# State times K and Q of a head in one 128-column block, and rows turned by VectorE from chunk 5 on

## The chip, the core and the metric

The kernel runs on one core of a Trainium2 chip. The core has five engines that follow their own instruction queues in order and wait for each other through semaphores: TensorE (matrix products, PE in the profile; its weight loads, which overlap the products, are PEld), VectorE (DVE), ScalarE (ACT), GpSimd (POOL) and SyncE (SP), which here issues nearly all DMAs. The metric is the device time of one execution in microseconds; a single execution has been profiled, and the times of three others are given as a median.

## What is computed

A delta-rule attention layer in float32 (4 batches, 8 heads, 768 steps, head size 48) feeds a gated feed-forward layer over 3072 tokens (model width 384, inner width 1536):

```python
for t in range(S):
    kt, vt, bt = (k_n[:, :, t], v[:, :, t], beta[:, :, t, None])
    y[:, :, t] = np.einsum('bhd,bhde->bhe', q[:, :, t], state)
    v_old = np.einsum('bhde,bhd->bhe', state, kt)
    state = state + bt[:, :, :, None] * np.einsum('bhd,bhe->bhde', kt, vt - v_old)
...
x = np.ascontiguousarray(attn_out.transpose(0, 2, 1, 3)).reshape(B * S, H * D)
...
rms = np.sqrt(np.mean(x * x, axis=-1, keepdims=True) + 1e-06)
xn = x / rms * rms_g
g = xn @ w_gate
silu = g * (1.0 / (1.0 + np.exp(-g)))
val = xn @ w_val
return (silu * val @ w_out).astype(np.float32)
```

`k_n` is k divided by its norm.

## The kernel before

The 768 steps are cut into 12 chunks (`NCH`) of 64 steps (`C`). The 32 pairs of batch and head lie as 16 columns of pairs, in two halves of the 128 partitions. For each chunk `c` the kernel runs these stages:

- `norms(c)` and `prep(c)`: the norms of K, K scaled (L816), K turned so that the head's dimension lies on the partitions (`kt`; from chunk 5, `KVEC`, by a trip through DRAM and a VectorE transpose of 32x32 blocks, L819 to L828; before that by TensorE transposes, L537), the scores of K with itself (`scores`, L560) and the inverse of a triangular matrix in 32x32 pieces (L865 to L930, with scaling by beta on GpSimd from chunk 4 on). Two merge products (L971, L991) join the pieces in `mt`; between them stands `zz`, which borrows a part of `yn`.
- `qpart(c)`: Q turned into `qt` (L625) and its scores with K (`pt`).
- `recur(c)`: the state times K (`on_state(kt)`, L1029) is taken from V into `r_` (L1058); the state times Q (`on_state(qt)`, the same line) is copied into `yn` (L1066). Then `mt` times `r_` gives `u_` (L1092), and `u_` gives both the second part of the output (`pu`, L1106) and the growth of the state (`ku`, L1163). `yn` is summed (L1194), its mean square taken (L1200), and scaled (L1233). TensorE turns it in three 128x128 transposes for each of two row groups (L1239), and ScalarE copies it with the factor `rms_g` into `xf` (L1248). Seven VectorE sums of `xf`'s parts follow (L1263).
- `ffn(c)`: from chunk 2 on, 30 groups of products (L1406) by a scheme with fewer products, with sums on VectorE and ScalarE (L1416 to L1423), and then `down` with seven products (L1463). Chunks 0 and 1 use plain products (`ffn_plain`, L1311 and `down_mm`, L1293). `xf` can be written for the next chunk once the last L1406 product has read it.

A matmul on a part of the array names its rows by the partitions of its operands and its columns by the partitions of its output. In `on_state` each product has 48 rows (one head's dimension, lower or upper half of the partitions by `d`) and 64 stationary columns (64 steps), with output on the lower or upper half by `bb`: four tiles of 64x64. Two neighbouring half columns of `kt` or `qt` belong to the heads `g` = 0 and 1.

What sets the order is a list. Each operation is added to a `Plan` with its engine, an estimated duration and the keys that it reads and writes. `ORDER` is a string of two digits per operation that names the sequence, and `Plan.run` writes the instructions of all engines out in that sequence; PSUM banks are handed out (`Group`) in the same walk. So each engine's queue is fixed when the program is built; the durations steer the hand-out of banks and the fillers at the start, and nothing at run time.

SyncE issues its DMAs one after the other; one that waits for its data holds up those behind it.

## Time and profile before

| what | value |
|---|---|
| median of three runs | 669.61 us (667.61 to 669.8) |
| the profiled execution, own time | 669.93 us |
| its span, first to last instruction | 668.2 us |
| granted TensorE clock | 0.999 |
| busy in the span: TensorE, its loads, VectorE, ScalarE, GpSimd | 656.6, 606.7, 530.3, 299.3, 147.5 us |
| records of L1029 (matmuls of the state with K or Q) | 704 + 640 |
| records of L1239 (transposes of yn) | 72 |
| instructions in the span | 23232 |

Busy times overlap between engines and do not add up. Each float32 matmul shows up as two records of matmul and two of weight load; a transpose leaves one. A record's duration holds its latency, so that records that follow each other closely overlap, and what a block of them costs is seen from the start of one block to the start of the next.

### The profile page before, as it was taken

The numbers are of one execution on the slowest core, as the hardware profiler recorded it, in microseconds if no ns is written. First come the engines' busy times: TensorE is split into PE (matmuls) and PEld (weight loads), VectorE is DVE, ScalarE is ACT, GpSimd is POOL, SyncE is SP. The second block draws the span as 40 slices with busy tenths as digits, with TensorE's granted clock in tenths as the row PEclk, the third lists the DMA queues.
The fourth block names the chain that finished last, engine by engine and source line by source line (L and its number), as shares of the span: only waits on it lengthen the run. The fifth ranks groups of instructions, "written<-read, shape, count | busy, mean of one in ns | idle before, by whom it ended". The sixth has DMA issues, their size and how long they took to land.

```text
span 668.2 us, 23232 instructions
## 1 busy us (share of the span) xinstructions
PE 656.6 (98%) x9970; PEld 606.7 (91%) x9970; DVE 530.3 (79%) x1139; ACT 299.3 (45%) x729; POOL 147.5 (22%) x204
## 2 busy tenths in 40 slices
PE   8989999999999999999999999999999999999997
PEld 5777787787899999999999999999999999999997
DVE  5888999888789798798898798698789699458263
ACT  4676734235246246346245346345345255245230
POOL 2211332032600600610710510610501401000000
PEclk9999999999999999999999999999999999999999
DMA  8489855766555176265356276174373601200101
GB/s 217 94 312 258 204 143 81 130 128 107 132 81 104 41 120 117 49 105 88 57 94 103 46 126 111 29 129 67 71 116 49 115 15 27 41 18 2 24 2 24
DMA packets 259799, 63.07 MB, mean 94 GB/s; under 512 B 248880, under 2 KB 251952, under 8 KB 259376
## 3 DMA queue, kind: packets, MB, share of 16 engines
q1 hardware_dynamic: 258656, 61.39, 46.7%
q8 instruction: 78, 1.28, 0.8%
q10 hardware_dynamic: 1040, 0.20, 0.2%
q14 instruction: 25, 0.20, 0.1%
HBM read 46.61 MB, written 18.87 MB: 98 GB/s over the span
## 4 chain that ended last, share of the span: by engine, by line
PE 93%; DVE 3%; issue 1%; ACT 1%; DMA 1%; POOL 0%; SPq 0%; POOLq 0%; ACTq 0%; DVEq 0%
PE bank L1406 41%; PE bank L1463 21%; PE bank L1311 9%; PE bank L1293 4%; PE bank L1029 3%; PE bank L560 3%; PE bank L1106 2%; PE bank L1092 2%; PE bank L779 1%; PE bank L1239 1%; PE bank L1163 1%; PE bank L798 1%; PE bank L1574 1%; PE bank L971 1%; PE bank L991 1%
## 5 line engine op out<-in xcount | busy, mean ns | idle before, releaser
L1406 PE MATMUL bank<-xf,w_in 128*128 128x128 f32 x1440 | 178.3, 276 | 0.3 <-ACT tmp L1418 0.3
L1406 PEld LDWEIGHTS bank<-xf,w_in 128*128 128x128 f32 x1440 | 169.4, 192 | 1.6 <-ACT tmp L1418 0.5
L1416 DVE TENSOR_TENSOR tmp<-tmp,bank 128x512 f32<-128x512 f32 x180 | 120.3, 682 | 48.5 <-PE bank L1406 35.8
L1406 PE MATMUL bank<-xf,more 128*128 128x128 f32 x960 | 123.5, 277 | 0.0
L1418 ACT COPY tmp<-bank 128x512 f32<-128x512 f32 x120 | 68.9, 586 | 110.6 <-PE bank L1406 67.2
L1406 PEld LDWEIGHTS bank<-xf,more 128*128 128x128 f32 x960 | 115.2, 192 | 2.0 <-DVE r L1058 0.2
L923 DVE TENSOR_REDUCE acc<-acc 128x30 f32<-128x90 f32 (+4 forms) x150 | 71.0, 473 | 5.2
L1422 ACT ACTIVATE tmp<-tmp 128x256 f32<-128x256 f32 x120 | 48.4, 416 | 54.2 <-DVE tmp L1416 53.8
L1463 PE MATMUL bank<-wo_sb,hf 128*128 128x192 f32 x360 | 63.9, 328 | 0.0
L1463 PEld LDWEIGHTS bank<-wo_sb,hf 128*128 128x128 f32 x360 | 58.1, 190 | 0.7 <-issue 0.2
L917 DVE TENSOR_TENSOR acc<-acc,at 128x60 f32<-128x60 f32 (+4 forms) x150 | 52.6, 351 | 3.8 <-POOL at L897 0.6
L1423 DVE TENSOR_TENSOR hf<-tmp 128x256 f32<-128x256 f32 x120 | 47.6, 421 | 4.0 <-ACT tmp L1422 3.6
L865 POOL TENSOR_TENSOR at<-at,beta_b 128x256 f32<-128x256 f32 x32 | 25.0, 811 | 113.1 <-DMA at<-dkk 113.1
L605 POOL TENSOR_TENSOR knrm<-ksum,half 128x16 f32<-128x16 f32 x11 | 32.2, 2929 | 75.1 <-DVE ksum L584 74.8
L943 POOL COPY acc<-acc 128x128 f32<-128x128 f32 x40 | 16.8, 449 | 108.5 <-DVE acc L923 106.7
L1311 PE MATMUL bank<-xp,w_in 128*128 128x256 f32 x144 | 33.7, 383 | 1.2 <-issue 0.9
L1293 PE MATMUL bank<-wo_sb,hf 128*128 128x384 f32 x96 | 33.8, 490 | 0.0
L1311 PE MATMUL bank<-xf,w_in 128*128 128x256 f32 x144 | 33.2, 383 | 0.0
L1472 DVE TENSOR_TENSOR tmp<-tmp,bank 128x192 f32<-128x192 f32 x30 | 10.4, 350 | 28.6 <-PE bank L1463 28.5
L1311 PEld LDWEIGHTS bank<-xp,w_in 128*128 128x128 f32 x144 | 26.6, 190 | 5.8 <-issue 1.3
L1311 PEld LDWEIGHTS bank<-xf,w_in 128*128 128x128 f32 x144 | 26.8, 190 | 4.3 <-issue 0.2
L1212 POOL TENSOR_SCALAR ms<-ms 128x2 f32<-128x2 f32 x11 | 3.7, 336 | 115.3 <-ACT bank L1200 115.2
(205 smaller groups left out, 1026.7 us busy)
## 6 DMA issues: line engine op xcount, KB each, us to landing
at<-dkk SPq DMA_DIRECT2D x20, 256.0 KB, 4.6
vt<-in_v_dram SPq DMA_DIRECT2D x24, 192.0 KB, 4.4
out_dram<-tmp SPq DMA_DIRECT2D x48, 96.0 KB, 2.2
k<-in_k_dram SPq DMA_DIRECT2D x23, 192.0 KB, 5.4
dks<-k SPq DMA_DIRECT2D x14, 256.0 KB, 2.9
kt<-dks SPq DMA_DIRECT2D x28, 128.0 KB, 3.5
more<-in_moe_w_gate_dram SPq DMA_DIRECT2D x4, 768.0 KB, 9.9
more<-in_moe_w_out_dram SPq DMA_DIRECT2D x4, 768.0 KB
```

The lines of the kernel that those rows point to most:

```text
L605: P.add("POOL", 2.95, lambda: nc.gpsimd.tensor_tensor(out=knrm[i2], in0=ksum[i2], in1=half, op=ALU.pow), pn, r=[("ksum", i2), "half"], w=[ ...
L865: eng.tensor_tensor(out=at_[:, j0:j1], in0=at_[:, j0:j1], in1=bt[:, None, :].to_broadcast([128, j1 - j0, W]), op=ALU.mult)
L917: nc.vector.tensor_tensor(out=acc[:, 1:3, 0:n, j + 2 : W].rearrange("p a i t -> p i a t"), in0=acc[:, old, 0:n, j : j + 2, None].to_broadc ...
L923: nc.vector.tensor_reduce(out=acc[:, new, 0:n, j + 2 : W], in_=acc[:, lo : lo + 3, 0:n, j + 2 : W].rearrange("p a i t -> p i t a"), axis=A ...
L1293: nc.tensor.matmul(po[p].t[:, 0:DM], hf[:, spot(f), 128 * p : 128 * p + 128], wo_sb[:, spot(f)], start=(f == f0), stop=(f == f1 - 1), skip ...
L1311: nc.tensor.matmul(ps.t[:, TOK * side : TOK * side + TOK], w_in[:, side, h_, 3 * t + i_, n : n + 128], x_[:, 2 * t : 2 * t + 2].rearrange( ...
L1406: nc.tensor.matmul(g.t[:, 128 * z : 128 * z + 128], fac[:, side, 128 * f : 128 * f + 128], xf[:, xs], start=(begin and z == 0), stop=False ...
L1416: P.add("DVE", V(512), lambda t=t, g=g: nc.vector.tensor_tensor(out=t, in0=t, in1=g.t, op=ALU.add), -1, r=[g], w=[tk], last=g)
L1418: P.add("ACT", A(512), lambda t=t, g=g: nc.scalar.copy(t, g.t), -1, r=[g], w=[tk], last=g)
L1422: P.add("ACT", A(256), lambda t=t: nc.scalar.activation(out=t[:, 0:256], in_=t[:, 0:256], func=ACTF.Silu), -1, w=[tk])
L1423: P.add("DVE", V(256), lambda t=t, f0=f0, p=p: nc.vector.tensor_tensor(out=hf[:, spot(f0) : spot(f0) + 2, 128 * p : 128 * p + 128], in0=t[ ...
L1463: nc.tensor.matmul(g.t[:, 0:192], a_[:, f], b_[:, f], start=(begin and f == 0), stop=(f == 5), skip_group_check=True)
```

## The change

Five things are changed.

1. `kt` (two buffers) and `qt` become three slots of one tensor `kqt`, with K in slot 0 or 2 by the parity of the chunk and Q in slot 1, so that a head's K and Q of a chunk lie side by side in 128 columns. From chunk 2 (`FUSE`) the two blocks of `on_state` become `on_both`: for each batch half `bb` a block of 16 matmuls with 48 rows and 128 stationary columns. One half of the output's partitions is the state times K, the other the state times Q. The subtraction into `r_` and the copy into `yn` are each done for each `bb` and `d`, on 64 partitions. From chunk 6 on (`c > XVEC`) the block also waits until `yn` has been turned. The loads that bring K's blocks back from DRAM are eight where they were four, of half the size.
2. From chunk 5 (`XVEC`) `yn` goes to DRAM and comes back in four loads, arranged in 32x32 blocks; one VectorE transpose writes `xf`, and three ScalarE operations multiply by `rms_g`. The transposes on TensorE remain in chunks 0 to 4. For this the columns of x are dealt to the three groups by remainder, and the rows of the gate and value weights and `rms_g` are loaded to fit.
3. The GpSimd operations at the start of the triangular inverse (from chunk 4 on) leave out the part left of the diagonal.
4. `zz` moves from `yn` into a part of `kk`.
5. `ORDER` is another sequence, over a changed list of operations.

```diff
+XVEC = 5
+FUSE = 2
...
-    kt = sbt("kt", [128, 8, 128], NKQ)
-    qt = sbt("qt", [128, 8, 128])
+    kqt = sbt("kqt", [128, 8, 2, 3, C])
+    kt, qt = [kqt[:, :, :, 0], kqt[:, :, :, 2]], kqt[:, :, :, 1]
...
-                    src = w.rearrange("(t p) c -> p t c", p=128)[:, :, c1 : c1 + 256]
+                    src = w.rearrange("(p t) c -> p t c", t=KT)[:, :, c1 : c1 + 256]
...
-                    src = dks[i2, d].rearrange("u (m t) e -> t (u m) e", t=W)[:, :, W * eh : W * eh + W]
-                    dma(ksq[W * a : W * a + W].rearrange("p (b e) -> p b e", e=W), src, pr, r=[("dks", i2, d)], w=ktk, dur=0.6, work=0.95)
+                    for m in range(2):
+                        src = dks[i2, d].rearrange("u (g m t) e -> m t (u g) e", g=2, t=W)[m][:, :, W * eh : W * eh + W]
+                        dma(ksq[W * a : W * a + W, :, W * m : W * m + W], src, pr, r=[("dks", i2, d)], w=ktk, dur=0.6, work=0.5)
...
         def scale(j0, j1):
-            eng.tensor_tensor(out=at_[:, j0:j1], in0=at_[:, j0:j1], in1=bt[:, None, :].to_broadcast([128, j1 - j0, W]), op=ALU.mult)
+            t0 = 0 if fast else j0
+            eng.tensor_tensor(out=at_[:, j0:j1, t0:], in0=at_[:, j0:j1, t0:], in1=bt[:, None, t0:].to_broadcast([128, j1 - j0, W - t0]), op=ALU.mult)
...
+            def on_both(bb, ps):
+                for x_ in range(4):
+                    for g in range(2):
+                        for d in range(2):
+                            rows, u, n = slice(64 * d, 64 * d + D), 4 * bb + x_, 96 * x_ + 48 * g
+                            nc.tensor.matmul(ps[d].t[:, n : n + 48], kqt[rows, u, g, ikq : ikq + 2].rearrange("e z t -> e (z t)"), state[rows, 2 * u + g])
+
+            for bb in range(2 if c >= FUSE else 0):
+                ps = psf[bb]
+                P.rows = 64
+                P.add("PE", 0.62, lambda bb=bb, ps=ps: on_both(bb, ps), pr, r=ktk + qk + sk, w=ps + rk + ([("yn", p) for p in range(2)] if c > XVEC else []), ps=ps, size=64)
+                P.rows = 128
+            for bb in range(2 if c >= FUSE else 0):
+                ps = psf[bb]
+                for d in range(2):
+                    cut = lambda t, d=d: by_d(t.rearrange("s h e -> s (h e)"), d)
+                    P.add("DVE", V(384), lambda d=d, bb=bb, ps=ps, cut=cut: nc.vector.tensor_tensor(
+                        out=cut(r_[low(bb)]), in0=cut(vt[low(bb)]), in1=ps[d].t[low(ikq), 0:DM].rearrange("s (x n) -> s x n", x=4), op=ALU.subtract,
+                    ), pr, r=[("v", bb), ps[d]], w=[("r", d)], last=ps[d])
+                for d in range(2):
+                    P.add("ACT", A(384), lambda d=d, bb=bb, ps=ps: nc.scalar.copy(
+                        by_d(yn[low(bb)].rearrange("s p n -> s (p n)"), d), ps[d].t[low(1 - ikq), 0:DM].rearrange("s (x n) -> s x n", x=4)
+                    ), py, r=[ps[d]], w=[("yn", p) for p in range(2)], last=ps[d])
             P.rows = 64
-            P.add("PE", 0.98, on_first if c == 1 else lambda: on_state(kt[ikq], psk), pr, r=ktk + sk, w=psk + rk, ps=psk, size=128)
+            c < FUSE and P.add("PE", 0.98, on_first if c == 1 else lambda: on_state(kt[ikq], psk), pr, r=ktk + sk, w=psk + rk, ps=psk, size=128)
...
-            for p in h:
+            if c >= XVEC:
+                ysq, xsq = yn.rearrange("s p n -> s (p n)"), xf[:, 0:6]
+                yk = [("yn", p) for p in h]
+                dma(dy[i2].rearrange("p s n -> s p n"), yn, px, r=yk, w=[("dy", i2)], dur=0.6, work=1.1)
+                for a in range(4):
+                    src = dy[i2].rearrange("p (m j) (a n) -> a j (p m) n", j=W, a=4)[a]
+                    dma(ysq[W * a : W * a + W].rearrange("j (z n) -> j z n", z=8), src, px, r=[("dy", i2)], w=yk, dur=0.6, work=0.4)
+                P.add("DVE", V(768), lambda: nc.vector.transpose(
+                    out=xsq.rearrange("p (t y) n -> p t (y n)", t=KT).rearrange("p t (z j) -> p t z j", j=W), in_=ysq.rearrange("j (z e t) -> j t z e", z=8, t=KT),
+                ), pxv, r=yk, w=xkeys, port=False)
+                for k_ in range(KT):
+                    P.add("ACT", A(256), lambda k_=k_: nc.scalar.mul(xsq[:, 2 * k_ : 2 * k_ + 2], xsq[:, 2 * k_ : 2 * k_ + 2], g_sb[:, k_ : k_ + 1]), pxv, r=["g"], w=[xkeys[1]])
+            for p in h if c < XVEC else ():
...
-                        nc.tensor.transpose(psx.t[:, 128 * t : 128 * t + 128], yn[:, p, 128 * t : 128 * t + 128], ident)
+                        nc.tensor.transpose(psx.t[:, 128 * t : 128 * t + 128], yn[:, p, t::KT], ident)
```

`low(a)` is the half `a` of the 128 partitions, `by_d` the heads of half `d`, `W` is 32, `KT` is 3, `D` 48, `DM` 384.

## The prediction

> **What bounds the kernel now.** I read the page's busy times first, then the chain that ended last, then the stretches of the span, then the groups of TensorE and the chain in order of time.

> ```profile
> PE 656.6 (98%) x9970; PEld 606.7 (91%) x9970; DVE 530.3 (79%) x1139; ACT 299.3 (45%) x729; POOL 147.5 (22%) x204
> ...
> PE 93%; DVE 3%; issue 1%; ACT 1%; DMA 1%; POOL 0%; SPq 0%; POOLq 0%; ACTq 0%; DVEq 0%
> ```

> TensorE is busy for 656.6 of 668.2 us, and 93% of the chain is its own. The stretches (span, PE, PEld, DVE) show where the 11.6 us of idle time are:

> ```profile
> 0.00:40.00 40.00, 36.66 (x655) 26.84 (x656) 29.14 (x84) 22.81 (x60) 11.08 (x19) 1.00 0.66 160
> 40.00:110.00 70.00, 66.31 (x1040) 53.80 (x1039) 64.56 (x136) 42.76 (x80) 16.56 (x13) 1.00 0.75 207
> ...
> 420.00:470.00 50.00, 50.00 (x879) 48.08 (x878) 39.45 (x86) 22.90 (x56) 14.13 (x20) 1.00 0.47 80
> ...
> 620.00:668.20 48.20, 43.98 (x340) 43.68 (x338) 22.05 (x42) 12.21 (x30) 0.00 (x0) 0.98 0.08 17
> ```

> They lie before 110 us and behind the last matmul. In the chunks from 2 on, which the change mostly touches, TensorE does not wait. A microsecond of its work there is a microsecond of time; work on other engines is free until it makes TensorE wait. VectorE has room: it stood 48.5 us before L1416, 28.6 before L1472 and 13.7 before L1151, each time for TensorE.

> So the question is what a fused block costs TensorE. These groups carry the answer (mean ns of one weight load):

> ```profile
> L1406 PEld LDWEIGHTS bank<-xf,w_in 128*128 128x128 f32 x1440 | 169.4, 192 | 1.6 <-ACT tmp L1418 0.5
> L1029 PEld LDWEIGHTS bank<-state,kt 48*64 48x64 f32 x640 | 10.3, 135 | 1.6 <-issue 0.8 <-ACT xf L1248 0.5
> L1163 PEld LDWEIGHTS bank<-u,k 64*48 64x48 f32 x640 | 8.2, 122 | 0.0
> L971 PEld LDWEIGHTS bank<-m1bd,kk 128*32 128x32 f32 x320 | 4.9, 109 | 2.0 <-issue 0.7 <-DMA at<-dkk 0.5 <-DVE acc L917 0.3
> L1239 PEld LDWEIGHTS bank<-ident,yn 128*128 128x128 f32 x72 | 8.3, 141 | 1.1 <-ACT yn L1233 0.6
> ```

> A matmul in float32 leaves two records, each with its load. Loads of 32, 48, 64 and 128 columns last 109, 122, 135 and about 191 ns: 0.8 to 0.9 ns a column whatever the rows, on about 82. A load lies under the matmul before it, so what counts is the distance between records. The chain (start, length, records) gives that:

> ```profile
> 31.24 1.99 PE bank L798 x64
> ...
> 440.39 1.08 PE bank L1106 x64
> 441.47 0.72 PE bank L1163 x64
> 442.19 8.23 PE bank L1406 x72
> 450.43 1.08 PE bank L1029 x64
> ...
> 463.87 0.66 PE bank L1239 x6
> ...
> 471.07 1.96 PE bank L1406 x16
> ```

> I call it a round when each tile of the array in use has taken one record. L1029, L1106 and L560 (1.09 us) have four tiles of 64x64 and 16 rounds: 1.08 us less some 0.1 at the change of tile shape is 61 ns a round, the same for 48 and 64 moving columns. L798 has two such tiles, 32 rounds, only 32 moving columns: 62 ns. So neither the stream nor the number of instructions sets the round. L1163 has four tiles and 48 moving columns like L1106, but 48 stationary ones: 0.72/16 = 45 ns. In chunk 0 the same line runs with 64 stationary columns, and the two can be set side by side in the timeline:

> ```profile
> 38.33 1.15 PE L1163 MATMUL bank<-u,k 64*64 64x48 f32 x64 [0.24 <-ACT qt L549]
> ...
> 349.86 0.94 PE L1163 MATMUL bank<-u,k 64*48 64x48 f32 x64
> ```

> Less the last record's 0.21 us and over 63 steps that is 14.9 against 11.6 ns, or 60 against 46 ns a round of four: 16 columns more cost 13 to 14 ns, 0.8 to 0.9 a column. The width of the stationary block sets the round.

> **The change, part by part.**

> *The fused product.* In chunks 2 to 11 two blocks of L1029 (32 matmuls, four tiles) become two of 16 matmuls with 128 stationary columns and 48 rows: two tiles, 16 rounds each. The number of rounds stays and the stationary block doubles. From 60 ns, 64 more columns at 0.8 give 111. L1406 has 128 stationary columns and records 8.23/72 to 22.33/200 = 114 to 112 ns apart, though its 128 moving columns could set that too. I take 16 x 111.7 + 0.13 at the shape change = 1.92 us, against 1.08. Bounds: 16 x 105 + 0.1 = 1.78 and twice L798's round, 16 x 124 + 0.13 = 2.11. Over 20 blocks: (1.92 - 1.08) x 20 = **+16.8 us** (14.0 to 20.6).

> [...]

> *x turned without TensorE.* Chunks 5 to 11 lose six L1239 transposes: 7 x 0.66 = **-4.6 us**. In their place stand a store of yn to DRAM, four loads, one 32x32-block transpose on VectorE and three ScalarE scalings. The transpose of 768 elements is bounded by L828 (1024 contiguous in 1236 ns: 0.93 us) and L706 (512 strided in 1066 ns: 1.6 us); I take 1.3. Cover: xf comes free with the last L1406 product of a chunk at 463.87, and the next chunk's first starts at 471.07, so 7.2 us of other TensorE work lie between. The chain in them is now 0.66 + 6 x 0.376 (L1248) + 2.8 (L1263, 5 x 0.425 + 2 x 0.326) = 5.7 us; it becomes 1.3 + 3 x 0.45 + 2.8 = 5.5. Cost nothing. The trip through DRAM lies ahead of it (96 KB out land in 2.2, 128 KB back in 3.5 us) and is free if yn is scaled some 6 us before xf; without that cover it adds up to 6 us a chunk.

> *VectorE, ScalarE.* The subtraction into r and the copy to yn double in number over half the partitions: 20 x 0.547 = 10.9 us VectorE, 20 x 0.476 = 9.5 us ScalarE. With 7 x 1.3 VectorE gains 20 us in 530; its 90 us of standing for TensorE hide them. ScalarE loses 42 x 0.376 and gains 21 x 0.45: -6.3. GpSimd's shortened triangle (L865, L892, L897, 54 us) saves some 16 us of an engine off the path: 0.

> *Queues.* Each chunk from 5 on issues nine DMAs more on SyncE: five for yn, and eight loads of K's blocks for four. At about 0.6 us that is 5.4 us of a 51 us period, in a queue that waits in order. A store of yn that waits for ScalarE holds up what stands behind it, the copies of dkk and dx and the loads of K; these feed VectorE's triangle, whose result TensorE wants half a period later. I take 0.

> *The wait.* From chunk 6 the fused block waits for yn to be turned. Behind it in TensorE's queue stand output products, and r, mt and the state update need its result. The turn starts when xf is free, and TensorE then has the 7.2 us above in other work: 0, or about 1.5 us a chunk if the block is placed too early.

> *Small.* The transposes left in chunks 0 to 4 read every third column of yn: 30 records, 0 to 0.11 us each by doubling: I take 0, upper bound 3.3. The repacked weight and gamma loads move the same bytes: 0. The new order shifts the start by an unknown amount, +-2 us, since 7 us of idle lie there.

> **Sum:** +16.8 - 4.6 = +12.2. The profiled execution took 669.93 us (span 668.2 and 1.7 around it), 0.3 above the median of the runs, 669.61. On the median: **681.8 us**. Its own range: 14.0 - 4.6 - 2 = +7.4 to 20.6 - 4.6 + 3.3 + 2 = +21.3, so 677 to 691.

> **Rivals.**

> *A, the stream decides.* If a 128-column load hid fully, a round would be the 48 moving columns. L1311 streams 256 in 2.59/12 = 216 ns, 0.84 a column, so 40 ns: a block of 16 x 40 + 0.1 = 0.74 us. -0.34 x 20 - 4.6 = -11.4: 658. It decides from loads below 40 ns. For it: half as many records. Against: L798's 62 ns with only 27 ns of stream.

> *B, fast wide load.* The transposes load 128 columns in 141 ns, not 191. If the fused block's loads did so, the round stays near 61 ns, the block at 1.08, and only the transposes are saved: 665. Against: every load outside a transpose lies on the slow line.

> *C, x late.* The turn waits for its trip through DRAM and TensorE stands 1.5 to 3 us before each product stage from chunk 5: 7 x 1.5 to 3 = +10 to +21 on 681.8: 692 to 703. Against: the 7.2 us; for: SyncE's queue waits in order.

> *D, the two row tiles do not overlap.* A round is 223 ns, a block 3.7: +52 - 4.6: 717. Four tiles overlap today, so hardly.

> **Chances.** Forecast 0.71; A 0.13; B 0.07; C 0.06; D 0.01; cancelling to nothing 0.02. A measurement of this kernel tells some 0.3% from no change (667.6 to 671.6). Faster: A and B and a little, 0.21; same 0.03; slower 0.76. The range reaches down over B to 663 and up to 691, and leaves out A and most of C and D.

> **What would show it.** The fused group with 48x128 loads near 190 ns and 32 records in 1.8 to 2.0 us of the chain; 0.74 is A, 1.08 is B, 3.7 is D. L1239 down from 72 to 30 records. No waits of TensorE beyond 1 us in the middle of the span; waits on xf or yn there are C. TensorE's busy time near 669. If the fused block takes under 1.3 us, the forecast is wrong.

## The result and the profile after

The changed kernel takes 713.47 us (median of four, 711.79 to 715.75), the kernel before beside it 668.61: a ratio of 1.0663, 95% interval 1.0642 to 1.0685. The profiled execution took 715.1 us, with a span of 713.2, 45.0 more than before. Slower was forecast, but by 12 us and not by 45, and the time lies outside the range. Some executions fall into a slower state; the times, ranges and ratios below are of the others, which leaves out one execution, of the doubled blocks.

The page of the changed kernel, in the rows that answer to those of before, with the granted clock in 40 slices:

```profile
PE 695.1 (97%) x9298; PEld 640.2 (90%) x9298; DVE 553.0 (78%) x1166; ACT 308.0 (43%) x728; POOL 140.2 (20%) x204
...
PEclk9989799899999999999999899999999899999999
...
PE 84%; DVE 9%; ACT 2%; DMA 2%; issue 1%; SPq 1%; POOL 0%; DVEq 0%; POOLq 0%; ACTq 0%
```

TensorE has fewer records and yet is busy 38.5 us longer; 26 more than the forecast's 669. Its idle time grew too, from 11.6 to 18.1 us, and VectorE has 9% of the chain where it had 3%. The new sight is the clock: before, all 40 slices stood at 9; now five do not. The stretches (span, PE, PEld, DVE, ACT, POOL, clock, DMA share, GB/s) put numbers on it:

```profile
0.00:40.00 40.00, 37.23 (x589) 26.21 (x590) 28.01 (x80) 20.76 (x51) 9.85 (x15) 0.97 0.77 194
40.00:110.00 70.00, 64.75 (x1015) 54.64 (x1015) 58.33 (x127) 40.57 (x77) 16.34 (x15) 0.89 0.70 185
110.00:160.00 50.00, 50.00 (x643) 39.51 (x644) 43.95 (x94) 18.65 (x50) 10.84 (x15) 0.93 0.56 107
...
370.00:420.00 50.00, 50.00 (x725) 48.22 (x724) 37.11 (x78) 21.81 (x53) 12.43 (x20) 0.93 0.56 95
420.00:470.00 50.00, 49.02 (x683) 46.42 (x685) 43.17 (x89) 21.57 (x51) 10.81 (x17) 0.97 0.51 92
660.00:713.20 53.20, 49.06 (x377) 48.63 (x375) 26.22 (x52) 14.41 (x34) 0.00 (x0) 1.00 0.07 16
```

Between 370 and 420 us TensorE is busy without a gap, and still the clock's mean is 0.93. The trace lists nine stretches at 0.50 in this span, 47.7 us together, each one, two or three times 3.41 us long. Three lie in the start (37 to 89 us, 17.1 us), one at 262.9 (3.4), and five begin during or right behind the wide blocks (126, 393, 454, 505 and 563 us; 27.3).

The groups of TensorE loads and of the new turn (out and in, shapes, count, busy, mean ns, idle before):

```profile
L1453 PEld LDWEIGHTS bank<-xf,w_in 128*128 128x128 f32 x1440 | 169.8, 193 | 4.5 <-ACT tmp L1465 2.6 <-issue 0.4 <-DVE tmp L1463 0.2
...
L1063 PEld LDWEIGHTS bank<-state,kqt 48*128 48x128 f32 x640 | 38.7, 196 | 2.1 <-issue 1.1 <-ACT xf L1280 0.2
...
L1280 ACT ACTIVATE xf<-xf,g_sb 128x256 f32<-128x256 f32 x21 | 9.8, 502 | 12.6 <-DVE xf L1276 12.6
...
L1276 DVE STREAM_TRANSPOSE xf<-yn 128x768 f32<-128x768 f32 x7 | 8.6, 1234 | 0.0
L1198 PEld LDWEIGHTS bank<-u,k 64*48 64x48 f32 x640 | 8.2, 122 | 0.3 <-DVE more L1418 0.3
...
L1286 PEld LDWEIGHTS bank<-ident,yn 128*128 128x128 f32 x30 | 4.2, 199 | 0.8 <-DVE u L1186 0.2
```

L1063 is the wide block: its loads of 128 columns last 196 ns. VectorE never stood idle for the data of L1276 to come back from DRAM (0.0), and no product of TensorE waits for `xf` from the turn; its weight loads for L1063 stood 0.2 us in all for L1280. The chain in order of time, from four places (start, length, records):

```profile
259.06 0.62 DVE acc L933
...
261.71 0.34 DVE hf L1470
...
262.13 0.59 ACT tmp L1465
...
262.77 4.59 PE bank L1453 x24
...
273.55 1.92 PE bank L1063 x32
...
339.42 3.71 PE bank L1063 x64
343.13 0.57 PE bank L1002 x16
...
389.49 4.11 PE bank L1063 x64
393.60 1.01 PE bank L1002 x16
394.61 4.14 PE bank L1510 x12
```

One wide block is 1.92 us, two that are neighbours 3.71. Behind the pair at 339 the next work goes on as it should: 0.57 us for the 16 records of L1002. Behind the pair at 389 the same 16 records take 1.01 us, and 12 of L1510 take 4.14, where at 301 us the same line has them in 2.16. That is work at half clock, and it was not in the sum at all. At 259 to 263 us the chain is VectorE's and ScalarE's: TensorE stands there for a bank, and behind it 24 records of L1453 take 4.59 us, where 2.7 is usual.

### The profile page after: what moved, and what is told of

Its sections match the earlier page's. It is cut to its first block, busy times and chain, and to the rows that moved or that the text cites. A ratio compares the mean times of both kernels' runs of the same rounds, so it can differ in the third digit from the quotient of the medians.

```text
span 713.2 us, 22037 instructions
## 1 busy us (share of the span) xinstructions
PE 695.1 (97%) x9298; PEld 640.2 (90%) x9298; DVE 553.0 (78%) x1166; ACT 308.0 (43%) x728; POOL 140.2 (20%) x204
## 4 chain that ended last, share of the span: by engine, by line
PE 84%; DVE 9%; ACT 2%; DMA 2%; issue 1%; SPq 1%; POOL 0%; DVEq 0%; POOLq 0%; ACTq 0%
PE bank L1453 31%; PE bank L1510 19%; PE bank L1358 9%; PE bank L1063 6%; PE bank L1340 4%; PE bank L565 3%; PE bank L1621 3%; DVE acc L933 2%; DVE tmp L1463 2%; DVE acc L927 2%; PE bank L1141 2%; PE bank L1127 1%; DVE hf L1470 1%; PE bank L803 1%; SPq L379 1%
## 5 line engine op out<-in xcount | busy, mean ns | idle before, releaser
L1453 PE MATMUL bank<-xf,w_in 128*128 128x128 f32 x1440 | 179.6, 277 | 2.0 <-ACT tmp L1465 2.0
L1453 PEld LDWEIGHTS bank<-xf,w_in 128*128 128x128 f32 x1440 | 169.8, 193 | 4.5 <-ACT tmp L1465 2.6
L1453 PE MATMUL bank<-xf,more 128*128 128x128 f32 x960 | 124.1, 278 | 3.4 <-ACT tmp L1465 2.4
L1453 PEld LDWEIGHTS bank<-xf,more 128*128 128x128 f32 x960 | 115.6, 193 | 5.6 <-ACT tmp L1465 3.0
L1465 ACT COPY tmp<-bank 128x512 f32<-128x512 f32 x120 | 68.6, 586 | 104.6 <-PE bank L1453 77.7
L1469 ACT ACTIVATE tmp<-tmp 128x256 f32<-128x256 f32 x120 | 47.7, 414 | 66.5 <-DVE tmp L1463 66.2
L933 DVE TENSOR_REDUCE acc<-acc 128x30 f32<-128x90 f32 (+4 forms) x150 | 70.9, 473 | 5.1
L1510 PE MATMUL bank<-wo_sb,hf 128*128 128x192 f32 x360 | 67.9, 342 | 0.4 <-DVE tmp L1463 0.3
L1510 PEld LDWEIGHTS bank<-wo_sb,hf 128*128 128x128 f32 x360 | 61.6, 200 | 1.8 <-DVE tmp L1463 0.5
L927 DVE TENSOR_TENSOR acc<-acc,at 128x60 f32<-128x60 f32 (+4 forms) x150 | 51.7, 345 | 3.5
L1470 DVE TENSOR_TENSOR hf<-tmp 128x256 f32<-128x256 f32 x120 | 48.5, 431 | 5.5 <-ACT tmp L1469 5.4
L1063 PEld LDWEIGHTS bank<-state,kqt 48*128 48x128 f32 x640 | 38.7, 196 | 2.1 <-issue 1.1
L1063 PE MATMUL bank<-state,kqt 48*128 48x48 f32 x640 | 40.4, 282 | 0.0
L1358 PE MATMUL bank<-xp,w_in 128*128 128x256 f32 x144 | 35.1, 397 | 2.5 <-ACT xf L477 2.5
L872 POOL TENSOR_TENSOR at<-at,beta_b 128x256 f32<-128x256 f32 (+3 forms) x32 | 18.8, 620 | 85.2 <-DMA at<-dkk 85.2
L1358 PEld LDWEIGHTS bank<-xp,w_in 128*128 128x128 f32 x144 | 28.1, 198 | 8.1 <-ACT xf L477 2.6
L953 POOL COPY acc<-acc 128x128 f32<-128x128 f32 x40 | 17.6, 472 | 86.9 <-DVE acc L933 86.3
L1358 PE MATMUL bank<-xf,w_in 128*128 128x256 f32 x144 | 34.5, 393 | 0.0
L1074 DVE TENSOR_TENSOR r<-vt,bank 64x384 f32<-64x384 f32 x40 | 21.3, 549 | 13.9 <-PE bank L1063 4.7
```

The costliest lines, as they stand in the source:

```text
L927: nc.vector.tensor_tensor(out=acc[:, 1:3, 0:n, j + 2 : W].rearrange("p a i t -> p i a t"), in0=acc[:, old, 0:n, j : j + 2, None].to_broadc ...
L933: nc.vector.tensor_reduce(out=acc[:, new, 0:n, j + 2 : W], in_=acc[:, lo : lo + 3, 0:n, j + 2 : W].rearrange("p a i t -> p i t a"), axis=A ...
L1063: nc.tensor.matmul(ps[d].t[:, n : n + 48], kqt[rows, u, g, ikq : ikq + 2].rearrange("e z t -> e (z t)"), state[rows, 2 * u + g])
L1358: nc.tensor.matmul(ps.t[:, TOK * side : TOK * side + TOK], w_in[:, side, h_, 3 * t + i_, n : n + 128], x_[:, 2 * t : 2 * t + 2].rearrange( ...
L1453: nc.tensor.matmul(g.t[:, 128 * z : 128 * z + 128], fac[:, side, 128 * f : 128 * f + 128], xf[:, xs], start=(begin and z == 0), stop=False ...
L1465: P.add("ACT", A(512), lambda t=t, g=g: nc.scalar.copy(t, g.t), -1, r=[g], w=[tk], last=g)
```

## The experiments

### One part of the change at a time, in the old order

Three kernels have the sequence of the kernel before, or nearly so. With `ORDER` as before, the first keeps the layout of K and Q side by side, the columns dealt to three groups, eight loads of K for four, the shortened triangle and the new place of `zz`, and drops the rest:

```diff
-XVEC = 5
-FUSE = 2
+XVEC = 99
+FUSE = 99
```

> The changed kernel without the fused block and without VectorE's turning of x (both switches set past the last chunk), in the order of the kernel before; what stays is the shared tensor of K and Q, eight loads of K's blocks for four, x's columns dealt by remainder, the shorter triangle on GpSimd and zz in kk. Theory S+O (what is lost besides the wide blocks is lost by the new order): as the kernel before, 669 (667 to 672). Theory L (the layout, the strided transposes or the extra loads cost): 674 to 685, with the loss in the start or behind waits on K.

669.38 us, ratio 1.0008 (0.9997 to 1.0018): all of this costs nothing, as the prediction had it. The second puts the wide block alone on top, one block in place of each block with K or Q:

```diff
 def on_state(t, ps):
     for x_ in range(4):
         for g in range(2):
             for d in range(2):
-                for bb in range(2):
-                    rows, u, n = slice(64 * d, 64 * d + D), 4 * bb + x_, 96 * x_ + 48 * g
-                    nc.tensor.matmul(ps[d].t[64 * bb : 64 * bb + 64, n : n + 48], t[rows, u, g], state[rows, 2 * u + g])
+                bb = 0 if ps is psk else 1
+                rows, u, n = slice(64 * d, 64 * d + D), 4 * bb + x_, 96 * x_ + 48 * g
+                nc.tensor.matmul(ps[d].t[:, n : n + 48], kqt[rows, u, g, ikq : ikq + 2].rearrange("e z t -> e (z t)"), state[rows, 2 * u + g])
```

> As the run in the old order, but the two blocks of state times K and state times Q of each chunk from 2 on (and Q's of chunk 1) are each one wide block of 16 matmuls with 48 rows and 128 stationary columns, at their old places, which mostly lie apart; so the outputs of heads are mixed up and only the work is that of the change. Theory S (loads set the block; two neighbouring blocks are needed for the low clock): 21 x 0.84 = 17.6 us on 669, about 687 (684 to 691), clock near 1. If every wide block drops the clock by itself: 700 or more. If the wide block were cheap and the new order the whole loss: 669.

687.49 us, 1.0286 (1.027 to 1.0301): 18.1 over the run without the wide block, for 21 blocks 0.86 us each, where 0.84 was forecast. The clock stays at 0.999. In its chain a block stands alone, between other work at full speed:

```profile
266.28 2.15 PE bank L1504 x12
268.43 0.57 PE bank L1000 x16
269.01 1.92 PE bank L1039 x32
270.93 1.17 PE bank L1504 x6
```

The third keeps the turn of x on VectorE and no wide block (`FUSE = 99`), with the old sequence up to some 195 us and one made for it from there:

> As the run in the old order, with VectorE's turning of x from chunk 5 on and without the fused block; from chunk 4 on the order is adapted so that yn is scaled early enough for the trip through DRAM. Theory S+O (the turn by itself saves its 42 transposes, 4.6 us, and hides its trip when the order allows for it): 669.4 less 4.6, about 665 (663 to 667), faster than the kernel before. Rival C (the trip through DRAM or the fuller queues cost wherever they stand): 670 or more, with waits of TensorE on xf or on banks from chunk 5 on.

666.66 us (10 runs), 0.997 (0.9956 to 0.9984): 2.4 us less than before in this batch, of the 4.6 forecast. TensorE's busy time fell by 3.5:

```profile
PE 653.1 (98%) x9928; PEld 602.3 (90%) x9928; DVE 545.0 (82%) x1146; ACT 297.1 (45%) x708; POOL 137.7 (21%) x204
```

Two new waits took most of the difference, 1.6 us of L563 and 0.7 of L1039. This is the only version of all that beats the kernel before, by about as much as can be told from no change.

So the parts, one by one, do what the sum said or come near: 0 for 0, +18.1 for 17.6, -2.4 for -4.6. The 30 us on top come from the parts together, or from the order.

### The new order with other blocks

The changed kernel, whole, but with the wide block split into four tiles of 64x64 as before, the order untouched:

```diff
-nc.tensor.matmul(ps[d].t[:, n : n + 48], kqt[rows, u, g, ikq : ikq + 2].rearrange("e z t -> e (z t)"), state[rows, 2 * u + g])
+for z in range(2):
+    nc.tensor.matmul(ps[d].t[64 * z : 64 * z + 64, n : n + 48], kqt[rows, u, g, ikq + z], state[rows, 2 * u + g])
```

> The changed kernel with its order and everything else as it is, but each fused block takes K and Q as two 64-column stationary blocks again (four tiles of 64x64, 32 matmuls, the same results in the same places). Theory S (the wide block costs its weight loads, 1.92 us for 1.08, and the stretches of half clock behind pairs of wide blocks come from it too): 16.8 us of work and some 13 us of half clock go, so 713.5 becomes about 683 (679 to 688), and the clock is at half only in the start. Theory O (the half clock comes from the new order's waits, not from the wide blocks): only the 16.8 us go, about 697, with the low stretches behind the blocks still there.

693.73 us, 1.0375 (1.0357 to 1.0393), between the two expectations. It tells two things. The wide blocks cost 19.7 us here. And without them the new order still costs 25 us over the kernel before, and 29 over what the saved transposes would give:

```profile
PE 667.3 (96%) x9938; PEld 613.2 (89%) x9938; DVE 552.5 (80%) x1166; ACT 308.0 (45%) x728; POOL 137.7 (20%) x204
...
PEclk9999799999999999999999999999999999999999
```

TensorE stands idle for 24.8 us, 13 more than before, and 20.5 us are at half clock, none of them behind a block with the state, except one at 600.6 us, where TensorE had stood for 1.5 us before the last records of that block. Where the order loses can be read from the start of the last product of L1453 (L1406 before) in a chunk: in chunk 2 it lies at 208.5 us before, 229.2 after, 221.9 in this run; in chunk 3 at 258.6, 290.3 and 281.5. Both lose most of it by then.

Next, the changed kernel with its wide loads as they are, but 96 moving columns for each matmul, so that each one also computes 48 columns that the next overwrites:

```diff
+w_ = 2 if 2 * u + g < 15 else 1
-nc.tensor.matmul(ps[d].t[:, n : n + 48], kqt[rows, u, g, ikq : ikq + 2].rearrange("e z t -> e (z t)"), state[rows, 2 * u + g])
+nc.tensor.matmul(
+    ps[d].t[:, n : n + 48 * w_], kqt[rows, u, g, ikq : ikq + 2].rearrange("e z t -> e (z t)"),
+    state[rows, 2 * u + g : 2 * u + g + w_].rearrange("p x e -> p (x e)"),
+)
```

> The changed kernel, but every wide matmul streams the next head's 48 columns of the state as well (96 for 48); what they leave is overwritten by the next matmul or never read. [...] Theory S (the clock gate watches how much the array streams, and a pair of wide blocks is 3.7 us of an array streaming a third of the time): the fused blocks stay at 1.9 us each, and the low clock behind pairs of them goes: about 700 (697 to 704). Theory O (the gate answers to waits of TensorE): clock and time as the changed kernel, 713. If the stream were what sets the block, it would grow by about 0.6 us a block: 725.

702.39 us, 1.0516 (1.0494 to 1.0538): twice the streaming, and 11 us less. None of the half clock behind the blocks is left; what stays is in the start (36.7 to 43.5, 81.0 to 84.4 us) and at 255. That the array streams a third of the time is an estimate from two measured numbers: 48 columns at the 0.84 ns of L1311 are 40 of the 112 ns of a round (1.79 us in 16). The pair itself takes the same 3.71 us with twice the stream, under loads of 188 ns, so its loads set the round:

```profile
489.08 0.58 PE bank L982 x32
489.66 3.71 PE bank L1064 x64
493.37 1.09 PE bank L565 x64
494.46 0.57 PE bank L1002 x16
```

### Another order for the whole change

The whole change with another sequence of the same 2857 operations, and the same with 96 moving columns. The sequence is that of the kernel before up to some 195 us and was made anew from there, with 1.82 us for a wide block (the changed kernel's plan counts 0.62):

```diff
 ORDER = (
-    "#.#'#(#&#*#3###w#+#4#$#-#0#/#T#U#C#`#W#>#^#a#_#X#V#2#k#)#Y#,#Z#d#l#b#n#m#e#o#H#c#t#E#f#[#]#r#u#q#v#x#R#?#y#D#j#z#p#="
+    "#.#+#-###'#3#4#)#0#$#(#%#/#*#w#>#`#W#C#^#a#T#_#&#X#U#k#,#Y#Z#d#l#b#n#m#o#c#t#e#H#V#f#u#[#]#s#v#x#r#S#y#q#R#z#1#{#=#|#J"
...
```

> The whole change as it is, fused block and turn, in another order: the start of the kernel before, and behind it one made with 1.82 us for a fused block where the changed kernel's plan has 0.62; all ten pairs of fused blocks stand next to each other. Theory S+O (16.8 us of loads, less 4.6 of transposes, and half clock behind pairs; the rest of the changed kernel's loss is its order): 669 + 12.2 = 681 plus half clock behind about half of the ten pairs, 1.7 to 3.4 us each, so 687 to 696. Theory C (the change costs TensorE waits whatever the order): 700 or more, with waits in the middle of the span.

> As the run of the whole change in the other order, but each wide matmul streams 96 columns for 48, as in the earlier run that did so. Theory S: no half clock behind the pairs, so 681 (679 to 685), which is the kernel before with the two terms of the sum alone, +16.8 and -4.6. If the low clock had to do with the width of the load and not with the stream, the same time as that run.

691.72 us, 1.035 (1.0311 to 1.039), and 685.56 us, 1.0254 (1.023 to 1.0279). So the order alone is worth 22 us of the 45, and what is left of them in the second, 16.5 us over the kernel before, is near the sum of the prediction: 685.6 for 681.8. In the first the clock is halved four times, each time behind two neighbouring blocks; in the second none of these is left, and the one halved period it has, at 52.4 us, lies in the start. The order's 22 us and the clock are not two separate sums: from the changed kernel's order to this one the half clock falls from 47.7 to 17.1 us, worth up to 15.3 of the 22.

### Repairs of the order, one after another

The changed kernel with the start of its sequence (up to entry 514 of 2857, 492 of them moved) put into the order of the kernel before, by the same kind of edit; all behind it is untouched:

> The changed kernel with the first 468 operations in the order of the kernel before (up to about 110 us), and the rest in its own order. Theory O (the new order's start loses 14 us, 8.5 of them at half clock, before and besides any fused block): 713.5 less 10 to 16, 698 to 704, with the low clock gone before 110 us. If the start's loss is only moved, because what follows waits for the same data: 710 to 715.

706.73 us, 1.0578 (1.0555 to 1.06). A gain of 6.7 us, less than the 10 to 16 expected. The half clock of the start (17.1 us) is gone, which is worth up to 8.5, and the profiled span is 8.8 us shorter. Behind the blocks there are 27.3 us at half clock, as many as in the changed kernel, at other places: the clock now halves behind two pairs that it had spared, at 157 and 215 us, and spares the one at 454. What the start loses besides its half clock came up again behind it: the last product of chunk 2 starts at 225.6 us for 229.2.

Then chunk 3 alone, around the stand at 259 us. VectorE does eleven of its fifteen solving steps (L927, L933) there without a break, from 251.4 to 261.7 us, and empties no bank meanwhile; only ScalarE goes on emptying some. The entries 885 to 1188 (293 of them moved) were put into another sequence, with the steps spread:

> The changed kernel with only the order of chunk 3 rearranged (some 300 of 2857 entries), so that the fifteen solving steps of VectorE (L927, L933) there no longer run in one go, but with evacuations of the product stages between them. Theory W (TensorE stood 12 us behind these steps between 250 and 263 us of the span, and its clock was halved for 3.4 us behind that): the stretch shrinks, no half clock in it, 5 to 9 us less than 713.5: 704 to 708. Rival M (VectorE's work is only moved, and TensorE stands for the same steps later): 712 to 715.

```profile
248.33 3.57 PE bank L1452 x32
251.90 1.95 PE bank L1509 x12
253.85 2.68 PE bank L1452 x24
256.53 1.92 PE bank L1062 x32
```

The stand is gone from this part of the chain, which is TensorE's throughout, and 24 records take 2.68 us. But the median, 712.36 us (709.6 to 715.63; ratio 1.0665, 1.0638 to 1.0691), is that of the changed kernel. From the last product of chunk 2 to that of chunk 3 the profile has 57.8 us for 61.1, so 3 us were won there, and in the four runs they do not show against the scatter. The half clock of this chunk was moved and not removed: it now stands at 230.1 us, behind a stand of 1.8 us in which TensorE waits for ScalarE's L1077 and VectorE's L1073. The 5 to 9 us that I expected from chunk 3 are not there; the time is that of rival M.

Last the two repairs and the 96 columns together:

> Three repairs of the changed kernel's order and clock at once: the entries up to the middle of chunk 2 as in the kernel before, chunk 3 with its solving steps spread, and the wide blocks with 96 moving columns in place of 48, so that TensorE streams while it loads. The wide blocks and the missing transposes stay. Theory T (the excess over the forecast is half clock behind the wide blocks, plus a bad start, plus chunk 3): no half clock behind the blocks or the start, and 669 + 17 for the wide loads - 2 to 4 for the transposes + 0 to 6 of small waits left = 682 to 690. Rival U (the repairs don't add up, because half clock and waits only come up elsewhere): 697 or more.

696.67 us, 1.0414 (1.0396 to 1.0431): above theory T's 690 and just short of rival U's 697. Of all half clock one stretch is left, 117.2 to 130.8 us, worth up to 6.8 us. The periods of 3.4 us before and in it:

```profile
113.80:117.20 3.40, 1.40 (x5) 0.68 (x4) 3.23 (x8) 0.86 (x2) 2.10 (x4) 0.99 0.63 79
117.20:120.60 3.40, 2.44 (x21) 2.06 (x20) 2.93 (x5) 2.07 (x6) 0.38 (x1) 0.50 0.95 154
```

TensorE is busy for 1.40 us of 3.40, since VectorE is again busy with solving steps, and the next period is at 0.50: here the clock follows an engine that stood idle for a part of the period, as it does in the changed kernel in the start and at 262.9 us:

```profile
34.20:37.60 3.40, 2.05 (x82) 1.92 (x80) 1.06 (x3) 0.58 (x2) 1.46 (x3) 1.00 0.35 125
37.60:41.10 3.50, 3.50 (x58) 2.99 (x51) 2.93 (x8) 2.43 (x11) 0.97 (x3) 0.51 0.62 180
...
259.45:262.87 3.42, 1.25 (x9) 1.07 (x9) 3.21 (x9) 1.10 (x2) 0.00 (x0) 1.00 0.76 116
262.87:266.28 3.41, 3.41 (x17) 3.41 (x18) 3.24 (x9) 0.86 (x2) 1.77 (x4) 0.51 0.00 0
```

The changed kernel lies 28 us over what its wide loads alone explain (668.6 + 16.8 = 685.4); repairs and stream together took 17 of these.

### What halves the clock

The old order, the wide block alone, and each block computed twice in a row, first with 48 moving columns and then with 96:

```diff
-                for x_ in range(4):
+                for x_ in (0, 1, 2, 3, 0, 1, 2, 3):
```

> The kernel before's layout and order with the wide block alone (both halves of its output mixed up, as in the run with the wide block alone), and each of the 21 wide blocks computed twice in a row into the same bank, so that 3.7 us of 128-column loads with 48 moving columns follow one another, as in the changed kernel where two blocks are neighbours. One block alone left the clock whole and the time at 687.5. Theory P (a doubled block is enough to halve the clock, whatever the order): 687.5 + 21 x 1.79 = 725, plus 1.7 to 3.4 us behind a third or more of the blocks: 737 to 760, with stretches at half clock that begin behind the blocks. Rival Q (it is the order of the changed kernel, its waits, and not the blocks): 723 to 728, and no half clock in the span.

> The same with 96 moving columns in place of 48, the loads unchanged (the outputs are mixed up as before). The block's time stays with its loads, 1.92 and 3.71 us. Theory P, if what halves the clock is how little TensorE streams: no half clock, 723 to 728. If the number or the width of the loads halves it, or the time in this tile shape, the same as its partner with 48 columns.

With 48 columns 753.9 us (743.32 to 754.05; 1.1218, 1.1134 to 1.1302), with 96 columns 725.46 (724.96 to 725.93; 1.0842, 1.0823 to 1.0861). The second is what 21 more blocks cost (687.5 + 21 x 1.79 = 725), with the clock at 1.00. The first streams half as much, loads the same, waits for nothing new, and takes 28.4 us longer, with 61.4 us of its profiled span at half clock. Two neighbouring periods of it, from one place where the clock fell and from one where it didn't:

```profile
440.91:444.33 3.42, 3.42 (x64) 3.42 (x62) 2.08 (x7) 0.00 (x0) 1.52 (x4) 1.00 0.00 0
444.33:447.74 3.41, 3.41 (x19) 3.34 (x18) 0.69 (x1) 2.29 (x7) 0.02 (x1) 0.50 0.50 87
...
239.55:242.96 3.41, 3.41 (x53) 3.19 (x53) 3.31 (x7) 0.00 (x0) 3.33 (x8) 1.00 0.02 5
242.96:246.37 3.41, 3.41 (x92) 3.30 (x91) 0.49 (x2) 1.53 (x3) 1.43 (x4) 1.00 0.00 0
```

```
block within a period          periods   next period at half clock
2.82 to 3.41 us of 3.41           11               11
2.47 to 2.70 us                    4                0
below 2.3 us                      20                0
```

At 440.91 the block fills the whole period and the next one is halved; at 239.55 it fills 2.70 us, and nothing happens. 11 of 21 blocks were hit. In the changed kernel, the one with another order and those of the two repairs with 48 columns, another 17 periods hold 2.85 us or more of wide block, and all are followed by a halved one; none below 2.4 us at full clock is. Between the two both occur: 2.80 us halved once and once not; what decides there was not found. With 96 moving columns ten periods of the doubled blocks hold 2.87 us or more, and none is followed by a halved one. So in these blocks it is the little streaming, and not the load or the tile shape, that halves the clock.

## Why the prediction was right and wrong

*Right: the fused block, to the second digit.* The term "16 x 111.7 + 0.13 at the shape change = 1.92 us" measured 1.92 (its bounds were 1.78 and 2.11). The loads last 196 ns, and with 96 moving columns the block still takes 1.92: the load sets the round, as was read from L1029, L1163 and L798. That settles rivals A (0.74 us), B (1.08) and D (3.7).

*Right: the transposes.* 72 records became 30; the distances from start to start of this group fell from 8.9 to 4.5 us. Alone, the turn gained 2.4 of the 4.6, since its order had new waits.

*Right: the cover of the turn, the queues and the wait.* The VectorE transpose takes 1.234 us (1.3 forecast), the scaling 0.50 (0.45), and no product of TensorE waits for either; rival C did not come. The trip lands in 2.4 us out and 2.4 back (2.2 and 3.5 forecast); that the first is so near is luck, since its price was read from stores of 96 KB and this one has 384. Of the 90 us that VectorE was said to stand for TensorE only 78 ended with it (35.8 of the 48.5 before L1416), which was room enough: VectorE grew by 22.7 us (20 forecast), ScalarE by 8.7 (3), and the layout cost 0 within the scatter.

*Wrong: "The new order shifts the start by an unknown amount, +-2 us, since 7 us of idle lie there."* That term was mis-sized, and it looked at the wrong place and the wrong quantity. The 7 us of idle bound what an order can win there, not what it can lose. A full order with the same operations is 22 us faster (713.5 to 691.7), and with narrow blocks the new order alone costs 25 over the kernel before. It loses by the end of chunk 2 (229.2 for 208.5 us) and in chunk 3 (61.1 us for 50.1). In the start the chain runs over two DMAs of weights and ScalarE's conversions of them (L477 and L478), and TensorE's L1358 goes on behind the first:

```profile
37.37 4.70 DMA wsum<-in_moe_w_val_dram
...
46.52 0.80 ACT xf L477
...
47.45 9.72 PE bank L1358 x36
...
69.83 6.30 DMA more<-in_moe_w_out_dram
```

The plan's 0.62 us for a block of 1.92 is one reason that was not looked at: a sequence sought with such a duration is sought for another kernel. That this is what made it bad was not tested. Two of the prediction's signs show the same: TensorE was busy for 695.1 us and not some 669, and at 262.8 us, in the middle of the span, it stood for 1.6 us, more than the 1 us that the sign allowed, though for ScalarE's L1465 and not for the turn.

*Missing: the clock.* Before, it was 0.999, so no term had it: the sum put it at nothing, while pairs of the wide blocks lower it. The profiled span grew by 45.0 us:

| part | us | from |
|---|---|---|
| 20 wide blocks | +16.8 | 1.92 for 1.08 |
| transposes | -4.4 | starts of the group |
| half clock, 47.7 us at half speed | up to +23.9 | of it 13.6 behind the blocks, 8.5 in the start, 1.7 at 263 |
| more idle time of TensorE | +6.5 | 18.1 for 11.6 |
| not assigned | +2.2 or more | |

The half clock's share behind the blocks was removed on its own: 11 us in the changed kernel, 6 in the other order, 28.4 with doubled blocks. The shares of the start and of the waits overlap with each other, and the repairs brought less than their rows: 6.7 and 1.1 us.

The changes of the clock lie on a grid of 3.41 us that the work does not move: of the nine stretches of the changed kernel, eight begin 3, 12, 26, 66, 104, 122, 137 and 154 periods behind the first. In the pairs of blocks TensorE was never idle, and the clock fell all the same: from 389.20 to 392.60 us it was busy for 3.40 of 3.40 us at 1.00, and the next 3.40 us stood at 0.50. Where the clock fell behind a stand of TensorE, the stand was shorter than a period of the grid: the longest of the changed kernel was 2.5 us.

*The chances.* 0.76 for slower was well placed, and not by luck, since the wide blocks alone, in the old order, cost 18 us; 663 to 691 was not: what the order may do was put at 2 us to either side, without a row that bounds it.

## What to carry to other kernels

Where the loads outlast the stream, as here (a round took 112 ns with 48 and with 96 moving columns), price a block of small matmuls by its loads, rounds times stationary columns; widening the stationary block to halve the instructions saved nothing here, where the number of rounds stayed (1.92 us for 1.08). Then ask how much TensorE streams while it loads: wide blocks with 48 moving columns that filled 2.82 us or more of a period of 3.41 us left 3.4 to 6.8 us at half speed behind them in these runs, a loss of 1.7 to 3.4 us, so put other products between two of them (with the blocks apart, in the old order, the clock stayed at 0.999). And when the sequence of a tuned kernel is made anew, treat it as a change of its own, with a range that the parts do not set, and test it with the old parts.

## What the runs showed of the hardware

- The clock of TensorE fell to half while TensorE was busy without a gap, when wide blocks with 128 stationary and 48 moving columns on 48 rows filled 2.82 us or more of a period of 3.41 us (28 periods in five kernels, all followed by a halved one). With 96 moving columns, the same loads and the same 3.71 us a pair, it stayed at 1.00 (724.2 us of span).
- Whether a pair is hit depends on how it falls into that grid: 11 of 21 doubled blocks were. The times of that kernel spread over 11 us (743.3 us at a mean clock of 0.970, 754.1 at 0.959), those of its partner with 96 columns over 1.
- In the run of doubled blocks a halved period was followed by another one where 0.86 us or more of a block lay in it, which made 6.8 us of the 3.4 in seven of eleven cases; with 0.09 us or none it was not. In the run with chunk 3 rearranged 0.81 us were not enough. Once halved by idle time, in the run with the repairs, the wide blocks with 96 columns did not bring it back: the pair took 7.07 us there.
- A tile of the array with 48 rows and 128 stationary columns loaded in 188 ns (the wide block alone in the old order, clock 0.999), about as one of 128 rows did (L1406 in the kernel before: 192).
